# Seventh head pair normalised by GpSimd inside its own unit and turned by DMA, and four blocks of the first product multiplied ahead of their Mish

## The chip, the cores and the metric

The kernel runs on one core of a Trainium2 chip. The metric is the device time of one execution in microseconds, lower is better. A run of this kernel is one program launch on real inputs. The engines are named as the profile names them: PE (TensorE, matrix products and transposes), PEld (its weight loads), DVE (VectorE), ACT (ScalarE), POOL (GpSimd), SP (SyncE, which here only issues DMAs).

## The reference

Attention over 8 batches, 12 heads, 448 positions, head size 64, with a softmax whose denominator has one more term, and then a two-layer network with the Mish function on all 3584 rows:

```python
scale = 1.0 / np.sqrt(q.shape[-1])
scores = scale * np.matmul(q, k.transpose(0, 1, 3, 2))
m = np.max(scores, axis=-1, keepdims=True)
e = np.exp(scores - m)
attn = e / (np.sum(e, axis=-1, keepdims=True) + np.exp(-m) + 1e-09)
attn_out = np.matmul(attn, v)
x = attn_out.transpose(0, 2, 1, 3).reshape(B * S, H * D)     # 3584 x 768
h = x @ w_in                                                 # 768 -> 2048
g = h * np.tanh(np.log1p(np.exp(np.minimum(h, 20.0))))       # Mish
out = g @ w_out                                              # 2048 -> 768
```

Inputs and output are fp32; inside, products take bf16 and sum in fp32.

## The kernel before

**Units.** Heads go in pairs (128 rows of q, k and v transposed together), six pairs to a batch, 48 in all. Pairs 0 to 5 (batch 0) form the head of the program. From then on three pairs make a unit: unit 2 is pairs 6, 7, 8, unit 3 is pairs 9, 10, 11, and so on to unit 15. Each unit has twelve steps (four per pair) and then a Mish part of eight blocks: half of the first product, with Mish, of the batch that is one behind. Unit 2 and unit 3 thus do blocks 0 to 7 and 8 to 15 of batch 0. From unit 4 on, the steps have the second product (`mm2_part`, L443) of earlier batches as filler on PE.

**A step.** `exps` (L298) takes the exponentials of a step's two row tiles on ACT (L306, one tile in a pair's last step), from PSUM into a bf16 buffer `en`, subtracting the row maximum. `scores_ahead` (L239) then lets PE compute scores up to three steps ahead, since there are three PSUM tiles `sc`, each free again after its exponentials. DVE reduces each to the negative maximum (L293). So a step turns around ACT, PE and DVE.

**After a pair.** `denominators` (L319, L323) and `normalise` (L325) divide `en` by the sum: seven row tiles, each one instruction, on DVE (L341) or on POOL (L339). For POOL's part, DVE first copies the reciprocals (L331). Then `en` has to be transposed to `eT`. There are two ways: a DMA transpose issued on SP's queue (L345), or `turn_on_pe` (L350), four turns of seven PE transposes each (L356), with an evacuation by DVE (L360). The list `BY_PE` names the pairs that PE turns: 2, 4, 5, 6, 7. `av_pair` (L368) multiplies `eT` with v (L382), and its result is copied to `xT` (L391), the input of the first product.

**The Mish part.** `mm1_mish` (L399) multiplies one block, six matmuls (L406), into a PSUM bank and takes Mish from it on ACT (L412). Between the blocks stand the denominators and normalisations of the unit's three pairs and the transposes (`transpose_pair`, L193) and evacuations (`evac_qk`; L214, L227, L235) of the next unit's three pairs of q and k. ACT has to load another table for Mish and again for the exponential, once each per unit. Before pairs 13 and 14, DVE clears buffers `qd` (L223, L224).

**Banks and evacuations.** Two PSUM banks `mo` serve the turns, the attention products and the blocks; the second block of each part uses an `sc` tile instead (`spare`). An evacuation is put on a list `late` and issued at the next step (`flush_late`).

**Order.** The schedule is written by hand: each engine runs its instructions in the order in which the code emits them, and so do the DMA queues of SP and POOL. `TURN_AT`, `AV_AT` and `W_AT` give for units 2 and 3 the step at which a turn, an attention product or a weight load is emitted. In unit 2, pair 8 was normalised first (DVE, then DMA), pair 6 after block 3 (DVE, then PE), pair 7 after block 4 (POOL, then PE); the turns of pairs 6 and 7 stood at steps 0 to 6 of unit 3, and their products at steps 5 and 8, that of pair 8 at step 10. The q, k and v loads (`load_pair`, L132) go on SP's queue at steps 0, 3 and 6, their casts to bf16 (L175, L176, L162) on POOL; the weights `w_in` and `w_out` come in pieces issued on POOL (L158).

Of the kernel before, what the change touches and what calls it, by code (L numbers as in the profile page):

```python
# [19 lines left out]
def kernel(  # L20
# [9 lines left out]
    nc = tc.nc  # L30
# [9 lines left out]
    FF_T = d_ff // 128  # L40
    NTILE = 2 * S // 128
    UNITS_PER_B = HP // UNIT_PAIRS
    N_UNITS = B * UNITS_PER_B
    HU = 2 * UNIT_PAIRS
    FF_U = FF_T // UNITS_PER_B
# [155 lines left out]
    def evac_qk(p, act=False):  # L201
        if p >= N_PAIRS:
            return
        (q_ps, k_ps), own = qkT[p]
        mo_free.extend(own)
        qd = q_diag[p % 3]
        kT = qk_pool.tile([128, S], BF16, tag="kT", name="kT")
        if not is_diag(p):
            qT = qd.rearrange("d i h r -> d (i h r)")[:, 0:S]
            qkT[p] = (qT, kT)  # L210
            if act:
                nc.scalar.mul(qT, q_ps[:, 0:S], SCALE)
            else:
                nc.vector.tensor_scalar(  # L214
                    out=qT, in0=q_ps[:, 0:S], scalar1=SCALE, scalar2=None, op0=ALU.mult
                )
            if p >= DIAG_FROM:
                nc.gpsimd.tensor_copy(out=q_rest[0:64, 0, :], in_=qT[0:64, 384:S])
                nc.gpsimd.tensor_copy(out=q_rest[64:128, 1, :], in_=qT[64:128, 0:64])
        else:  # L220
            qkT[p] = (qd, kT)
            if p < DIAG_FROM + 3:
                nc.vector.memset(qd[0:64, :, 1, :], 0.0)  # L223
                nc.vector.memset(qd[64:128, :, 0, :], 0.0)  # L224
# [73 lines left out]
    def exps(idx):  # L298
        p, s = divmod(idx, STEPS)
        if p >= N_PAIRS:  # L300
            return
        st = att[p]
        sc, cols = st.pop(("sc", s))
        rg["used"] -= 1
        for bk, c in enumerate(cols):
            nc.scalar.activation(  # L306
                out=st["en"][:, :, c, 0:SP_],
                in_=sc[:, bk, 0:S].rearrange("q (j c) -> q j c", j=NT),
                func=AF.Exp, bias=st["negm"][:, c : c + 1], scale=1.0,
                accum_out=st["sums"][:, c : c + 1],  # L310
            )
        if s == STEPS - 1 and p < HP:
            nc.scalar.activation(out=st["expm"], in_=st["negm"], func=AF.Exp)
        elif s == STEPS - 1 and p % UNIT_PAIRS == UNIT_PAIRS - 1:
            w = st["whole"]
            nc.scalar.activation(out=w["expm"], in_=w["negm"], func=AF.Exp)
# [8 lines left out]
    def normalise(p, dma=True, on_pool=False, shared=0):  # L325
        st = att[p]
        en = st["en"]
        if on_pool or shared:

            st["rden2"] = st_pool.tile([128, NTILE], FP32, tag="rden2", name="rden2")  # L330
            nc.vector.tensor_copy(out=st["rden2"], in_=st["rden"])  # L331
        for i in range(NTILE):
            pool_does = on_pool or i < shared
            args = dict(
                out=en[:, :, i, 0:SP_], in0=en[:, :, i, 0:SP_],
                scalar1=st["rden2" if pool_does else "rden"][:, i : i + 1],
            )
            if pool_does:
                nc.gpsimd.tensor_scalar(scalar2=1.0, op0=ALU.mult, op1=ALU.mult, **args)  # L339
            else:  # L340
# [55 lines left out]
        del att[p], casted[p], qkT[p]  # L396


    def mm1_mish(b, ff):  # L399
        if ff == 0:  # L400
            gT[b] = gT_pool.tile([128, FF_T, S], BF16, tag="gT", name="gT")
        flush_late()
        spare = ff % FF_U == 1
        h_ps = sc_tiles[0][:, 0, :] if spare else mo_take()
        for dm in range(DM_T):
            nc.tensor.matmul(  # L406
                h_ps[:, 0:S],
                lhsT=w_in_sb[:, dm, ff * 128 : (ff + 1) * 128],
                rhs=xT[b][:, dm, :],
                start=(dm == 0), stop=(dm == DM_T - 1),  # L410
            )
        nc.scalar.activation(out=gT[b][:, ff, :], in_=h_ps[:, 0:S], func=AF.Mish)  # L412
        if not spare:
            mo_free.append(h_ps)
# [78 lines left out]
    for g in range(B // 2):  # L493
# [12 lines left out]
        else:  # L506
# [6 lines left out]
    LEAD = UNIT_PAIRS + 1  # L513
    LOAD_AT = (0, 3, 6)
    LAST_AV_AT = (0, 6, 9)
    HEAD = HP

    BY_PE = (2, 4, HEAD - 1, HEAD, HEAD + 1)
    TURN_AT = (
        {0: [(4, 2)], 1: [(4, 3)], **{3 + j: [(HEAD - 1, j)] for j in range(NT)}},  # L520
        {0: [(HEAD, 0), (HEAD, 1)], 1: [(HEAD, 2)], 2: [(HEAD, 3)],
         3: [(HEAD + 1, 0)], 4: [(HEAD + 1, 1)], 5: [(HEAD + 1, 2)], 6: [(HEAD + 1, 3)]},
    )
    TURN_HEAD = {
        (3, 2): [(2, 0)], (3, 3): [(2, 1)], (4, 0): [(2, 2)], (4, 1): [(2, 3)],
# [1 line left out]
    }  # L527
    AV_HEAD = {(3, 3): 0, (4, 2): 2, (4, 3): 1}
    W_HEAD = {0: 3, 1: 1, 3: 1, 4: 1}
    AV_AT = ({3: 4, 7: 3, 9: 5}, {5: 6, 8: 7, 10: 8})  # L530

    W_AT = ({5: 1, 9: 1}, {1: 1, 4: 1, 5: 1, 7: 1, 9: 1, 11: 1}, {3: 1, 5: 1, 7: 1, 9: 1})
    for which in ("qk", "v"):
        for p in range(UNIT_PAIRS):
            load_pair(p, which)
# [39 lines left out]
    for u in range(UNITS_PER_B, N_UNITS + 2 * UNITS_PER_B):  # L575
# [10 lines left out]
        for n in range(steps):  # L586
# [22 lines left out]
            if u - UNITS_PER_B < len(AV_AT):  # L609
                early = AV_AT[u - UNITS_PER_B]  # L610
                if n in early:
                    av_pair(early[n])
                if u == UNITS_PER_B:
                    for part in TURN_AT[0].get(n, []):
                        turn_on_pe(*part)
            elif u == N_UNITS and n in LAST_AV_AT:
                av_pair(p0 - UNIT_PAIRS + LAST_AV_AT.index(n))
            if u - UNITS_PER_B < len(W_AT):
                load_w(W_AT[u - UNITS_PER_B].get(n, 0))
        assert done == total  # L620
# [63 lines left out]
```

## Time and profile before

| what | us |
|---|---|
| median of 3 runs | 481.12 |
| lowest and highest run | 479.0, 483.71 |
| the profiled execution | 479.95 |
| its span | 478.0 |

The profile is of one execution; its page has the time within the span, and 1.95 us of the execution lie around it. More of the page, the slices of the span (40 of 11.95 us each, a digit is a tenth of busy time) for the engines other than PE, and the costliest groups that the change touches (line, engine, operation, output and input, count, busy us in all and ns of one, and the idle time of the engine before them):

```profile
DVE  4888987968787886878687878788787869420021
ACT  5979678878787888979787878888897978412300
POOL 4877809255514334353535242433535340300000
...
L406 PE MATMUL mo<-xT,w_in_sb 128*128 128x448 bf16 x672 | 137.7, 353 | 0.6 <-DVE xT L391 0.6
L412 ACT ACTIVATE gT<-mo 128x448 bf16<-128x448 f32 x112 | 61.3, 547 | 68.2 <-PE mo L406 68.1
...
L339 POOL TENSOR_SCALAR en<-en,rden 128x448 bf16<-128x448 bf16 x122 | 76.4, 646 | 80.7 <-DVE rden L331 76.9
...
L341 DVE TENSOR_SCALAR en<-en,rden 128x448 bf16<-128x448 bf16 x214 | 58.6, 345 | 0.9
```

The mean of a PE instruction includes the fill of the array; matmuls follow each other closer than their duration. The stages meant below: the head up to 54 us, unit 2's steps to 65.0, its Mish part to 75.3, unit 3's steps to 92.2, its Mish part to 102.9, then unit 4 and on.

### The profile page before, as it was taken

The page shows a single profiled execution, that of the slowest core. Times are in us where ns is not written, and L with a number is a line of the kernel's source. Part 1 is how long each engine was busy: PE and PEld are TensorE (multiplying, and loading weights), DVE is VectorE, ACT ScalarE, POOL GpSimd, SP SyncE. Part 2 cuts the span into 40 slices and gives each one's busy share as a digit, 9 for nine tenths or more (in the row PEclk, how much of TensorE's full clock was granted, in tenths as well). Part 3 has the DMA queues.
Part 4 walks back from the last instruction along what each step waited for, and adds up shares of the span by engine and source line. Part 5 has one row for each costly group of instructions (what it writes and reads, how often), then busy time and mean ns, then how long its engine had stood idle before and what let it go on. Part 6 is the DMA issues. An engine that isn't in the chain of part 4 may idle for free.

```text
span 478.0 us, 8924 instructions
## 1 busy us (share of the span) xinstructions
PE 443.1 (93%) x3064; PEld 248.6 (52%) x3064; DVE 339.1 (71%) x680; ACT 350.0 (73%) x919; POOL 181.1 (38%) x315
## 2 busy tenths in 40 slices
PE   4565888898999999999999999999999999999997
PEld 2233544454655555555555555556555555556565
DVE  4888987968787886878687878788787869420021
ACT  5979678878787888979787878888897978412300
POOL 4877809255514334353535242433535340300000
PEclk9998798899999999999999999999999999999999
DMA  8999969999999989899999999899989595870113
GB/s 228 220 233 220 235 100 234 162 187 238 207 217 276 206 212 219 213 203 246 193 250 182 225 167 228 211 207 234 201 233 212 156 178 127 135 164 24 43 28 105
DMA packets 202381, 90.37 MB, mean 189 GB/s; under 512 B 159072, under 2 KB 198880, under 8 KB 202336
## 3 DMA queue, kind: packets, MB, share of 16 engines
q1 hardware_dynamic: 194848, 83.51, 81.3%
q0 software_dynamic: 7488, 6.29, 8.6%
q8 instruction: 24, 0.39, 0.3%
q14 instruction: 21, 0.17, 0.1%
HBM read 45.61 MB, written 11.01 MB: 118 GB/s over the span
## 4 chain that ended last, share of the span: by engine, by line
PE 76%; ACT 10%; DVE 9%; issue 2%; DMA 1%; POOL 0%; SPq 0%; DVEq 0%; ACTq 0%; POOLq 0%
PE mo L472 26%; PE mo L406 25%; ACT en L306 9%; PE sc L382 6%; DVE negm L293 6%; PE sc L266 5%; PE sc L406 4%; PE sc L193 3%; PE sc L272 2%; PE mo L356 1%; PE mo L382 1%; DVE en L341 1%; PE sc L280 1%; DVE eT L360 1%; DMA k_f<-in_k_dram 1%
## 5 line engine op out<-in xcount | busy, mean ns | idle before, releaser
L306 ACT ACTIVATE en<-sc,negm 128x448 bf16<-128x448 f32 x336 | 209.6, 637 | 26.4 <-DVE xT L391 10.4
L293 DVE TENSOR_REDUCE negm<-sc 128x2 f32<-128x896 f32 x192 | 180.7, 968 | 55.8 <-PE sc L275 26.0
L472 PE MATMUL mo<-w_out_sb,gT 128*128 128x384 bf16 (+1 forms) x912 | 142.3, 301 | 0.0
L406 PE MATMUL mo<-xT,w_in_sb 128*128 128x448 bf16 x672 | 137.7, 353 | 0.6 <-DVE xT L391 0.6
L412 ACT ACTIVATE gT<-mo 128x448 bf16<-128x448 f32 x112 | 61.3, 547 | 68.2 <-PE mo L406 68.1
L472 PEld LDWEIGHTS <-gT 128*128 128x128 bf16 x912 | 84.1, 98 | 48.2 <-issue 5.7
L339 POOL TENSOR_SCALAR en<-en,rden 128x448 bf16<-128x448 bf16 x122 | 76.4, 646 | 80.7 <-DVE rden L331 76.9
L406 PEld LDWEIGHTS <-w_in_sb 128*128 128x128 bf16 x768 | 72.9, 98 | 64.0 <-issue 3.0
L306 ACT ACTIVATION_READ_ACCUMULATOR en<-sc,negm 128x1 f32 x336 | 69.3, 206 | 0.0
L175 POOL CAST q_bf<-q_f 112x512 bf16<-112x512 f32 x47 | 29.0, 617 | 98.4 <-DMA q_f<-in_q_dram 98.0
L341 DVE TENSOR_SCALAR en<-en,rden 128x448 bf16<-128x448 bf16 x214 | 58.6, 345 | 0.9
L459 DVE COPY o_sb<-mo 128x384 f32<-128x384 f32 (+1 forms) x65 | 32.2, 495 | 35.1 <-PE mo L472 34.8
L266 PE MATMUL sc<-kT,qd 128*128 128x448 bf16 x168 | 47.7, 354 | 0.3 <-ACT en L306 0.2
L272 PE MATMUL sc<-kT,qd 64*128 64x448 bf16 x72 | 25.1, 411 | 12.7 <-ACT en L306 11.1
L382 PE MATMUL sc<-eT,v_bf 112*64 112x448 bf16 x288 | 34.1, 357 | 1.9 <-ACT en L306 1.7
L162 POOL CAST v_bf<-v_f 112x512 bf16<-112x512 f32 x48 | 29.5, 616 | 9.7 <-DMA v_f<-in_v_dram 8.8
L382 PEld LDWEIGHTS <-v_bf 112*64 112x64 bf16 x384 | 21.0, 112 | 22.8 <-issue 13.6
L176 POOL CAST k_bf<-k_f 112x512 bf16<-112x512 f32 x47 | 28.9, 616 | 7.5 <-DMA k_f<-in_k_dram 7.0
L227 DVE TENSOR_SCALAR qd<-sc 64x448 bf16<-64x448 bf16 x48 | 18.7, 389 | 11.9 <-PE sc L193 11.2
L266 PEld LDWEIGHTS <-qd 128*128 128x128 bf16 x168 | 16.3, 97 | 18.0 <-issue 9.2
L275 PE MATMUL sc<-kT,qd 64*128 64x448 bf16 x72 | 25.4, 415 | 0.0
L472 PE MATMUL mo<-w_out_sb,mid 128*128 128x384 bf16 x128 | 24.9, 326 | 0.0
(57 smaller groups left out, 340.1 us busy)
## 6 DMA issues: line engine op xcount, KB each, us to landing
q_f<-in_q_dram SPq DMA_DIRECT2D x48, 224.0 KB, 5.1
k_f<-in_k_dram SPq DMA_DIRECT2D x48, 224.0 KB, 5.4
v_f<-in_v_dram SPq DMA_DIRECT2D x48, 224.0 KB, 5.7
w_in_sb<-in_moe_w_in_dram POOLq DMA_DIRECT2D x12, 256.0 KB, 6.1
w_out_sb<-in_moe_w_out_dram POOLq DMA_DIRECT2D x8, 384.0 KB, 7.6
out_dram<-o_sb SPq DMA_DIRECT2D x7, 336.0 KB, 3.3
out_dram<-o_sb SPq DMA_DIRECT2D x8, 288.0 KB, 4.6
out_dram<-o_sb SPq DMA_DIRECT2D x8, 240.0 KB, 2.9
```

Source lines behind the costliest of these rows:

```text
L162: nc.gpsimd.tensor_copy(out=casted[p][2], in_=loaded.pop(p)[2])
L266: nc.tensor.matmul(sc[:, bk, 0:S], lhsT=qT[:, i].rearrange("d h r -> d (h r)"), rhs=kT, start=True, stop=True,)
L272: nc.tensor.matmul(sc[:, 0, 0:S], lhsT=qT[0:64, qa : qa + 128], rhs=kA, start=True, stop=True)
L293: nc.vector.tensor_reduce(out=negm, in_=sc[:, 0 : len(cols), 0:S], axis=AX.X, op=ALU.max, negate=True)
L306: nc.scalar.activation(out=st["en"][:, :, c, 0:SP_], in_=sc[:, bk, 0:S].rearrange("q (j c) -> q j c", j=NT), func=AF.Exp, bias=st["negm"][ ...
L339: nc.gpsimd.tensor_scalar(scalar2=1.0, op0=ALU.mult, op1=ALU.mult, **args)
L341: nc.vector.tensor_scalar(scalar2=None, op0=ALU.mult, **args)
L382: nc.tensor.matmul(av[h * 64 : (h + 1) * 64, 0:S], lhsT=v_bf[:, h, j * D : (j + 1) * D], rhs=e_h, start=(j == 0), stop=(j == NT - 1),)
L406: nc.tensor.matmul(h_ps[:, 0:S], lhsT=w_in_sb[:, dm, ff * 128 : (ff + 1) * 128], rhs=xT[b][:, dm, :], start=(dm == 0), stop=(dm == DM_T - 1),)
L412: nc.scalar.activation(out=gT[b][:, ff, :], in_=h_ps[:, 0:S], func=AF.Mish)
L459: nc.vector.tensor_copy(out=o_sb[:, cols], in_=st["o"][:, 0:n_cols])
L472: nc.tensor.matmul(st["o"][:, 0:n_cols], lhsT=src[:, ff, c0 : c0 + 128], rhs=w_out_sb[:, ff, cols], start=(ff == 0), stop=(ff == FF_T - 1),)
```

## The change

1. Pair 6 (`HEAD`) leaves `BY_PE`. At step 9 of unit 2 its denominators are computed (its own exponential of the negative maximum is added on ACT after its fourth step), POOL normalises it, and a DMA transpose on SP's queue turns it. Pair 8 stays with DVE and DMA; pair 7 is normalised by POOL after block 1 in place of block 4 and is turned by PE, now at steps 1 to 4 of unit 3.
2. The products of pairs 6, 8 and 7 stand at steps 1, 3 and 6 of unit 3, in place of 6, 7, 8 at steps 5, 8, 10.
3. Blocks 8 to 11 of batch 0 are multiplied at steps 5, 7, 8 and 10 of unit 3 (`mm1_ahead`). DVE copies each result to an fp32 tile in SBUF, and in the Mish part ACT takes Mish from there. The Mish part's order becomes 8, 12, 9, 13, 10, 14, 11, 15: one block ready, one multiplied.
4. The clearing of the two `qd` buffers moves from DVE to POOL, at the end of unit 3's steps. One weight load moves from block 2 of unit 2 to its step 9.
5. For pair 0, DVE does its three row tiles before it copies the reciprocals for POOL.

```diff
-            if p < DIAG_FROM + 3:
-                nc.vector.memset(qd[0:64, :, 1, :], 0.0)
-                nc.vector.memset(qd[64:128, :, 0, :], 0.0)
...
-        if s == STEPS - 1 and p < HP:
+        if s == STEPS - 1 and p <= HEAD:
             nc.scalar.activation(out=st["expm"], in_=st["negm"], func=AF.Exp)
...
-        for i in range(NTILE):
+        order = list(range(NTILE))
+        if shared and p == 0:
+            order = order[shared:] + order[:shared]
+        for i in order:
+            if i == 0 and (on_pool or shared):
+                for_pool()
...
+    def mm1_ahead(b, ff):
+        h_ps = mo_take()
+        mm1(b, ff, h_ps)
+        h_sb = o_pool.tile([128, d_model], FP32, tag="o_sb", name="o_sb")
+        h_sbs[b, ff] = h_sb
+        def evac():
+            nc.vector.tensor_copy(out=h_sb[:, 0:S], in_=h_ps[:, 0:S])
+            mo_free.append(h_ps)
+        late.append(evac)
+
+    def mm1_mish(b, ff, spare):
...
+        if (b, ff) in h_sbs:
+            nc.scalar.activation(out=gT[b][:, ff, :], in_=h_sbs.pop((b, ff))[:, 0:S], func=AF.Mish)
+            return
...
-    BY_PE = (2, 4, HEAD - 1, HEAD, HEAD + 1)
+    BY_PE = (2, 4, HEAD - 1, HEAD + 1)
     TURN_AT = (
...
-        {0: [(HEAD, 0), (HEAD, 1)], 1: [(HEAD, 2)], 2: [(HEAD, 3)],
-         3: [(HEAD + 1, 0)], 4: [(HEAD + 1, 1)], 5: [(HEAD + 1, 2)], 6: [(HEAD + 1, 3)]},
+        {1 + j: [(HEAD + 1, j)] for j in range(NT)},
...
-    AV_AT = ({3: 4, 7: 3, 9: 5}, {5: 6, 8: 7, 10: 8})
-    W_AT = ({5: 1, 9: 1}, {1: 1, 4: 1, 5: 1, 7: 1, 9: 1, 11: 1}, {3: 1, 5: 1, 7: 1, 9: 1})
+    AV_AT = ({3: 4, 7: 3, 9: 5}, {1: 6, 3: 8, 6: 7})
+    FIRST_AT = {5: FF_U, 7: FF_U + 1, 8: FF_U + 2, 10: FF_U + 3}
+    SECOND = [ff for i in range(4) for ff in (FF_U + i, FF_U + 4 + i)]
+    W_AT = ({5: 1, 9: 2}, {1: 1, 4: 1, 5: 1, 7: 1, 9: 1, 11: 1}, {3: 1, 5: 1, 7: 1, 9: 1})
...
+                if u == UNITS_PER_B + 1 and n in FIRST_AT:
+                    mm1_ahead(0, FIRST_AT[n])
...
+            if (u, n) == (UNITS_PER_B, 9):
+                denominators(att[HEAD])
+                normalise(HEAD, on_pool=True)
...
+        if u == UNITS_PER_B + 1:
+            for t_ in q_diag[1:]:
+                nc.gpsimd.memset(t_[0:64, :, 1, :], 0.0)
+                nc.gpsimd.memset(t_[64:128, :, 0, :], 0.0)
...
+        if u == UNITS_PER_B:
+            todo = [p0 + 2, None, p0 + 1]
         for f in range(FF_U):
             if moe:
-                mm1_mish(b, w * FF_U + f)
-            if u == UNITS_PER_B and f in (2, 6):
+                mm1_mish(b, SECOND[f] if u == UNITS_PER_B + 1 else w * FF_U + f, spare=f == 1)
+            if u == UNITS_PER_B and f == 6:
                 load_w(1)
...
-            if f == 3:
+            if f == 3 and todo[1]:
                 normalise(todo[1], dma=todo[1] not in BY_PE)
-            if f == 4:
+            if f == (4 if todo[1] else 1):
                 normalise(todo[2], dma=todo[2] not in BY_PE, on_pool=True)
```

More of the change, by code (lines that the diff above doesn't have):

```diff
@@ L42 @@
     UNITS_PER_B = HP // UNIT_PAIRS
+    HEAD = HP
     N_UNITS = B * UNITS_PER_B
@@ L327, in normalise, with for_pool @@
         en = st["en"]
-        if on_pool or shared:
+        def for_pool():
             st["rden2"] = st_pool.tile([128, NTILE], FP32, tag="rden2", name="rden2")
             nc.vector.tensor_copy(out=st["rden2"], in_=st["rden"])
-        for i in range(NTILE):
+        order = list(range(NTILE))
[4 more added lines that the diff above has]
+                for_pool()
             pool_does = on_pool or i < shared
@@ L396, in av_pair, with mm1 @@
         del att[p], casted[p], qkT[p]
[L399 to L404, printed above, removed]
+    def mm1(b, ff, h_ps):
         for dm in range(DM_T):
@@ L411, in mm1_mish @@
             )
+    h_sbs = {}
+    def mm1_ahead(b, ff):
[8 more added lines that the diff above has]
+    def mm1_mish(b, ff, spare):
+        if ff == 0:
+            gT[b] = gT_pool.tile([128, FF_T, S], BF16, tag="gT", name="gT")
+        flush_late()
+        if (b, ff) in h_sbs:
+            nc.scalar.activation(out=gT[b][:, ff, :], in_=h_sbs.pop((b, ff))[:, 0:S], func=AF.Mish)
+            return
+        h_ps = sc_tiles[0][:, 0, :] if spare else mo_take()
+        mm1(b, ff, h_ps)
         nc.scalar.activation(out=gT[b][:, ff, :], in_=h_ps[:, 0:S], func=AF.Mish)
@@ L515 @@
     LAST_AV_AT = (0, 6, 9)
-    HEAD = HP
-    BY_PE = (2, 4, HEAD - 1, HEAD, HEAD + 1)
+    BY_PE = (2, 4, HEAD - 1, HEAD + 1)
     TURN_AT = (
         {0: [(4, 2)], 1: [(4, 3)], **{3 + j: [(HEAD - 1, j)] for j in range(NT)}},
-        {0: [(HEAD, 0), (HEAD, 1)], 1: [(HEAD, 2)], 2: [(HEAD, 3)],
-         3: [(HEAD + 1, 0)], 4: [(HEAD + 1, 1)], 5: [(HEAD + 1, 2)], 6: [(HEAD + 1, 3)]},
+        {1 + j: [(HEAD + 1, j)] for j in range(NT)},
     )
```

## The prediction

> **What bounds the kernel now.** I read the page first (busy shares, then the 40 slices), then a table of busy time by stage, then the chain of waits around 86 to 104 us, then the timeline of single engines there.
>
> ```profile
> PE 443.1 (93%) x3064; PEld 248.6 (52%) x3064; DVE 339.1 (71%) x680; ACT 350.0 (73%) x919; POOL 181.1 (38%) x315
> PE   4565888898999999999999999999999999999997
> PEclk9998798899999999999999999999999999999999
> ```
>
> From the tenth slice on (about 119 us) TensorE has no idle time to speak of; before it, it waits. The change edits only work before 103 us and leaves later work as it is. So the question is when unit 4 begins: what is won or lost there is carried by a full TensorE to the end, nearly one to one. The 28 transposes taken away are worth nothing by themselves if they lay in TensorE's idle time.
>
> The stages (from and to, length, busy time of PE, PEld, DVE, ACT and POOL, granted clock, DMA share, GB/s): unit 2's Mish part, unit 3's steps, unit 3's Mish part, unit 4's steps.
>
> ```profile
> 65.00:75.30 10.30, 10.30 (x77) 5.44 (x76) 7.37 (x23) 6.68 (x12) 3.08 (x5) 1.00 0.67 143
> 75.30:92.20 16.90, 12.59 (x99) 7.41 (x98) 14.69 (x22) 15.14 (x47) 11.39 (x19) 0.80 1.14 214
> 92.20:102.90 10.70, 10.70 (x78) 5.79 (x76) 7.31 (x27) 6.93 (x13) 3.25 (x7) 0.99 0.85 151
> 102.90:119.40 16.50, 14.57 (x98) 8.14 (x97) 14.16 (x19) 15.04 (x45) 9.33 (x16) 1.00 1.09 227
> ```
>
> Both Mish parts are full on PE alone; unit 3's steps are nearly full on DVE and ACT, with PE idle 4.3 of 16.9 us at a mean clock of 0.80. Moving four blocks from a PE-full stage into a stage where PE has room is what the change can win. The chain of waits agrees:
>
> ```profile
> 88.64 2.84 PE mo L382 x16
> 91.48 1.67 PE mo L406 x6
> 93.16 1.13 PE sc L406 x6
> 94.29 0.40 PE sc L193 x8
> 94.68 2.27 PE mo L406 x12
> ```
>
> Every step from 88.64 to 102.3 is PE: two attention products at half clock, then eight blocks at about 1.14 us each (2.27 for two) with three transposed pairs (0.40) between them.
>
> **The change part by part.**
>
> *Unit 3's Mish part.* It ran from the table load at 92.17 to the next at 102.89, 10.7 us. After it, PE has 4 blocks x 1.14 + 3 x 0.40 + 0.66 for three scores = 6.4 us. ACT has the load 1.28, eight Mish at a 0.44 pitch and three copies of kT at 0.42 (starts 120.74, 121.18, 121.60, 122.01) = 6.1. That a Mish reads fp32 from SBUF instead of PSUM is in no row; the rows of 128x448 run 0.53 to 0.65 on ACT from either kind of source, so -0.1 to +0.1 each, and I take 0. DVE has 0.47 for the denominators, two normalisations at 1.81, evacuations 0.39 + 2 x 0.78 and 0.17, 6.2; its four memsets (0.245 each) have gone to GpSimd, idle for 8.29 us before 94.98, where four cost 0.8 (by the 0.20 memset) to 2.6 (by a 0.62 cast): hidden. Three engines near 6.3 do not mesh perfectly: 6.6. Gain 4.1.
>
> *Unit 3's steps.* DVE sets the pace there:
>
> ```profile
> 84.61 0.61 DVE L293 TENSOR_REDUCE negm<-sc 128x1 f32<-128x448 f32 x1
> 85.14 0.61 DVE L360 COPY eT<-mo 112x896 bf16<-112x896 bf16 x1
> 85.68 1.08 DVE L293 TENSOR_REDUCE negm<-sc 128x2 f32<-128x896 f32 x1
> 86.67 0.61 DVE L391 CAST xT<-mo 128x448 bf16<-128x448 f32 x1
> 87.20 0.61 DVE L360 COPY eT<-mo 112x896 bf16<-112x896 bf16 x1
> 87.74 2.61 DVE L293 TENSOR_REDUCE negm<-sc 128x2 f32<-128x896 f32 x3
> ```
>
> Starts follow each other without a gap: 1.0 us per double reduction, 0.53 per copy. Eleven copies stay eleven (four eT of pair 6 out, four h copies in; a 128x448 fp32 copy is between the 0.55 of a 128x384 fp32 copy and the 0.615 of the xT cast: 0.6, pitch 0.53). But their places change. From the reduction at 78.61 to the unit's last reduction (end 90.35) there were seven copies; in the new order there are nine (four eT, three xT, two h): +1.06. Pair 6's product now stands at step 1, when PE has just been idle and runs at half clock (1.71 us for the eight matmuls at 53.13 against 0.95): the evacuation behind it leaves DVE idle some 0.6. Against this, the last exponential began 0.95 after its reduction because ACT had its own queue; that slack goes. Net +0.06 + 1.06 + 0.6 - 0.95, plus some 0.2 of hand-over: +1.0. PE at full clock fits: four blocks at 1.14 come in, four turns of 0.55 to 0.99 go.
>
> *Unit 2.* The new denominators of pair 6 stand on DVE between the last reduction (63.26) and the xT copy of pair 5 (63.79). Their three instructions took 0.51 from first start to the next instruction at 43.07. Behind that copy wait the sixth matmul of the first block (64.46) and all blocks queued behind it, which run without a gap to 74.7: +0.5. The extra exponential of pair 6 (0.23) stands where ACT waits for DVE: 0. GpSimd normalises pair 6 from about 64.9 (seven at 0.62: to 69.2), where it was idle until 72.22.
>
> GpSimd and DVE then normalise side by side. The trace has this in the head, where DVE's third instruction took 0.633 against 0.328 while GpSimd's ran: it waited until GpSimd's ended. So I price pair 8's seven DVE instructions at one per GpSimd instruction, 7 x 0.62 = 4.4 us for 1.81. They end at 70.2, the evacuation behind them at 70.6, and PE's scores that need it were at 70.07, now 70.6: cost 0 by a hair, since the 1.81 us of pair 6 no longer stands on DVE. Pair 7's scalars are copied behind these, so GpSimd starts pair 7 at 70.8 and ends at 75.2 (before: 76.55).
>
> The Trainium skill's page "SBUF — State Buffer", section "Who interferes with whom", says that the two engines share one port pair as an exclusive lock and that the second to issue blocks for the whole instruction; the head's row agrees for DVE, and by the rule GpSimd would block in its turn, which is the third rival below.
>
> *Queues.* SP, in order: pair 6's transpose waits for GpSimd until 69.3, takes 4.2 (as at 67.42), pair 8's follows to 77.7; the loads behind them, at 71.72 before, come 6.0 later. GpSimd waits for them at pair 13's cast, done near 84.3 (3.3 to 4.6 us after issue, as at 108.77; before 81.3); behind it the last w_in piece lands 6.1 to 9.4 later, 90.4 to 93.7, needed by PE near 93.5: 0. Pair 0's reordering starts GpSimd 0.8 later, its transpose 0.8 later, its user stands 6 us after the landing: 0. Pair 6's own transpose lands near 75.8 to 78, its product is at 80.6: 0.
>
> *Unit 4.* The three transposes of unit 3 were issued at 95.03, 99.6 and 104.2 and landed 6.2 later; the products using them ran at 105.67, 111.06 and 115.99: slack 4.4, 5.3, 5.6. Transposes move by +1.5, products by -2.6: slack 0.3, 1.2, 1.5. I take a wait of 0.1.
>
> Sum: +0.5 + 1.0 - 4.1 + 0.1 = -2.5 us. The profiled execution took 479.95 (span 478.0 and 1.95 around it), so 477.5 of its kind; it lay 1.2 under the median of 481.12, against which I state the forecast: 478.6.
>
> **The rivals.**
>
> *No stretch.* DVE's new copies fit into gaps, and unit 2's delay is absorbed in ACT's 1.28 table load: -4.1 to -4.6. For it: ACT idles 2.2 us in unit 3's steps. Against: DVE's gapless starts above. Time 476.7.
>
> *Late transposes in unit 4.* Landing took 9.3 at 121.87 instead of 6.2, with other transfers about; here w_out pieces, issued some 5 us later, would be those. The first product then waits 3.0 beyond its 0.3 slack, the later ones not more: -2.5 + 2.8 = +0.3, 481.4.
>
> *Lock both ways.* GpSimd also waits for DVE (its first instruction beside DVE took 0.725, not 0.639). Seven pairs at 0.62 + 0.25 end at 71.8 and the scores behind run 1.5 late: -1.0, 480.1.
>
> *Half clock through unit 3's steps (slower).* PE now idles from 75.2 to 78.6, longer than the 2.1 us after which the clock showed 0.50 to 0.61 from 78.3 to 81.7; from 46.0 to 54.5 it stayed at 0.50 for 8 us with PE mostly busy. If that holds over the steps, four blocks cost 1.14 more each (4.6), three turns 0.43 (1.3), seven scores 0.2 (1.4), two products 0.54 (1.1): +8.4, nearly all on the path since PE would be full. -2.5 + 8.4 = +5.9, 487. It turns the sign when it holds for over 30% of the stretch, some 3.4 us past 82.4. Against it: PE has no gap over 0.4 us in the new order from 78.6 on.
>
> The Trainium skill's page "TensorE: Matmul & The Clock Gate", section "What's actually happening", says that the clock returns after one busy window of about 3.4 us which runs freely; by that rule, an estimate, the half clock would end between 82 and 85.4 and cost at most 2.5, the whole gain. The chain above has a half-clock stretch end near 92.5 after some 4 us.
>
> **How the numbers follow.** Forecast 0.52, no stretch 0.20, late transposes 0.12, lock 0.07, half clock 0.09. Runs of one kernel spread from 479.0 to 483.71, so 1% (4.8 us) is about what a measurement tells from no change. Faster by over 1% means under 476.3: half of "no stretch" and a sixth of the forecast, 0.19. Slower by over 1% means above 485.9: the half clock and some of the late transposes with the spread, 0.13. Within: 0.68. The range 475.5 to 483.5 takes in all but the half clock and the tails, with the spread of the runs.
>
> **What would show it.** Right: the stretch between the two table loads around unit 3's Mish part falls from 10.7 to about 6.6; the last reduction of unit 3's steps ends near 92.5; the first matmul of the output product at 100.4 instead of 102.89; two transposes on SP's queue back to back from 69.3 and the loads from 77.7. Wrong: a gap before a product in unit 4 that a transpose ends; PEclk at 5 after 85; a gap on PE near 70 to 73; DVE idle in unit 3's steps. The forecast falls if the steps stretch by more than 3 us or not at all.

## The result, and the profile after

| | changed kernel | kernel before, on the same chip |
|---|---|---|
| median of 9 runs each, us | 485.17 | 480.25 |
| lowest and highest, us | 484.28, 487.82 | 479.0, 483.71 |
| ratio, 95% interval | 1.011 (1.0082 to 1.0138) | |
| the profiled execution, its span | 486.29, 484.3 | 479.95, 478.0 |

The change costs 1.1%, about 5 us, where the prediction said 478.6 and gave a range up to 483.5. The page of the changed kernel, its busy shares and the slices for PE and its clock:

```profile
PE 444.0 (92%) x3036; PEld 246.9 (51%) x3036; DVE 341.1 (70%) x672; ACT 350.4 (72%) x920; POOL 186.7 (39%) x326
PE   4565887988879999999999999999999999999996
PEclk9998797999989999999999999999999999999999
```

The sum of PE's work is the same within 1 us, and the clock of unit 3's steps no lower than before. In PE's row the seventh to twelfth slices now read 7, 9, 8, 8, 8, 7 where before they read 8, 8, 9, 8, 9, 9; the twelfth (133 to 145 us) has an 8 in the row of the clock as well, for a 9. The last two of these slices lie in units 4 and 5, which the diff does not touch.

The table by stage of the changed kernel (from and to, length, busy time and instructions of PE, PEld, DVE, ACT and POOL, granted clock, DMA share, GB/s); the lines are unit 2's Mish part, unit 3's steps, its Mish part, unit 4's steps, its Mish part, and unit 5's steps:

```profile
65.30:76.90 11.60, 10.74 (x73) 5.50 (x73) 7.89 (x16) 6.88 (x12) 10.68 (x18) 1.00 0.63 93
76.90:95.20 18.30, 15.47 (x97) 7.45 (x97) 14.36 (x21) 15.30 (x46) 9.24 (x16) 0.81 1.19 227
95.20:102.10 6.90, 6.16 (x51) 3.43 (x50) 6.29 (x23) 6.66 (x14) 1.48 (x5) 1.00 1.35 175
102.10:119.50 17.40, 14.85 (x98) 8.18 (x98) 14.17 (x20) 15.04 (x45) 8.29 (x14) 1.00 1.07 235
119.50:130.30 10.80, 9.56 (x72) 5.13 (x70) 8.24 (x23) 6.89 (x14) 7.20 (x14) 1.00 1.26 207
130.30:151.10 20.80, 18.35 (x114) 9.85 (x113) 14.12 (x19) 15.21 (x45) 5.02 (x9) 0.92 1.10 218
```

The stages begin and end with ACT's table loads. By the exact loads, in us, where M is a Mish part, S a unit's steps and the number the unit:

| | M2 begins | M2 | S3 | M3 | S4 | M4 | S5 | M5 |
|---|---|---|---|---|---|---|---|---|
| before | 64.99 | 10.35 | 16.83 | 10.72 | 16.55 | 9.32 | 16.77 | 9.97 |
| changed | 65.27 | 11.64 | 18.31 | 6.86 | 17.46 | 10.72 | 20.87 | 9.89 |
| difference | +0.28 | +1.29 | +1.48 | -3.86 | +0.91 | +1.40 | +4.10 | -0.08 |

The differences add up to +5.5, and the last table load of the program indeed comes 5.5 us later (412.04 against 406.51). From unit 6 on the stages of the two kernels are alike. The spans of the two profiles differ by some 6.2 us; the other 0.7 lies behind the last matmul (4.0 us to the end for 3.3) and was not followed. So unit 3's Mish part gave what was promised (-3.86 for -4.1), units 2 and 3 gave back 2.8 of it, and units 4 and 5 took 6.4 more. Unit 5 is the largest item. The chain of waits of the changed kernel leads there (start, length, what):

```profile
97.97 7.66 DMA eT<-en
...
120.94 2.88 DVE en L345 x6
123.82 0.07 DVE qd L215
123.89 12.13 DMA eT<-en
...
136.16 0.95 PE sc L386 x8
```

The first DMA transpose of unit 4's pairs is issued at 123.89 and lands 12.1 us later; unit 5's first attention product waits for it. Before, the same transpose was issued at 121.87, took 7.2 us of SP's queue and landed after 9.3, at 131.2, and its product ran at 132.15 without an idle time in front of it:

```profile
132.15 0.95 PE L382 MATMUL sc<-eT,v_bf 112*64 112x448 bf16 x8
```

A stretch of the second product fills PE up to that point. So the first product had a slack of about 1 us, which the prediction does not weigh. The second had none left: its transpose landed at 137.01 and it ran at 137.15. The same stretch of the changed kernel in narrow windows:

```profile
134.00:136.20 2.20, 0.04 (x2) 0.07 (x4) 0.00 (x0) 1.46 (x6) 0.00 (x0) 1.00 1.21 256
136.20:138.00 1.80, 1.80 (x12) 0.90 (x13) 0.48 (x1) 0.00 (x0) 0.00 (x0) 0.80 1.17 218
138.00:140.00 2.00, 2.00 (x8) 0.86 (x6) 1.13 (x3) 0.73 (x2) 0.00 (x0) 0.50 1.08 199
140.00:142.00 2.00, 2.00 (x11) 1.00 (x10) 1.85 (x3) 1.33 (x4) 0.00 (x0) 0.83 1.15 215
```

PE is empty for the 2.45 us of the wait, runs its product at full clock, and then stands at 0.50 from about 137.3 to 140.7: 3.4 us at half clock, which costs 1.7 us of PE's work. 2.45 + 1.7 = 4.15, against 4.10 more in unit 5's steps. The Trainium skill's page "TensorE: Matmul & The Clock Gate", section "What's actually happening", gives a free-running window of about 3.4 us for the clock, and puts the drop after one idle window. The half clock here has that length, but 2.45 us of idle time were enough for it, and the drop came 1.1 us after PE had work again.

Why the transpose takes longer is in SP's queue (start, length, instruction; three transposes each, those of unit 3's pairs and of unit 4's). Before:

```profile
95.03 13.69 SPq L345 DMA_TRANSPOSE eT<-en  x3
...
121.87 16.58 SPq L345 DMA_TRANSPOSE eT<-en  x3
```

Changed:

```profile
97.97 14.35 SPq L349 DMA_TRANSPOSE eT<-en  x3
...
123.89 18.75 SPq L349 DMA_TRANSPOSE eT<-en  x3
```

The second of unit 3's in the kernel before (at 99.91), with no load and no weight piece in flight beside it, takes 4.3 us of the queue and lands after 6.2; three take about 13. Behind unit 3's three stand, in order, nine loads (pairs 16 to 18; from 108.77 before, from 112.36 now), POOL's casts of them, and behind the casts on POOL the last four pieces of `w_out` (issued two at a time, at 115.09 and 118.30 before, at 118.71 and 122.00 now). The last two, before and changed:

```profile
118.30 1.48 POOL L158 DMA_DIRECT2D w_out_sb<-in_moe_w_out_dram  x2
```

```profile
122.00 1.48 POOL L159 DMA_DIRECT2D w_out_sb<-in_moe_w_out_dram  x2
```

When unit 4's first transpose was issued, all nine loads had landed, and of the pieces three were in flight before and four now. Before, the last two were 3.6 us old; now they were 1.9 us old. The last piece landed at 128.2 before and at 133.5 now, and the transpose 3.0 and 2.5 us after it.

### The profile page after: what moved, and what is told of

Same layout as the page of the kernel before. It is cut to its first block, busy times and chain, and to the rows that moved or that the text cites. A ratio compares the mean times of both kernels' runs of the same rounds, so it can differ in the third digit from the quotient of the medians.

```text
span 484.3 us, 8864 instructions
## 1 busy us (share of the span) xinstructions
PE 444.0 (92%) x3036; PEld 246.9 (51%) x3036; DVE 341.1 (70%) x672; ACT 350.4 (72%) x920; POOL 186.7 (39%) x326
## 4 chain that ended last, share of the span: by engine, by line
PE 71%; DVE 12%; ACT 9%; DMA 5%; issue 2%; SPq 0%; DVEq 0%; ACTq 0%
PE mo L496 26%; PE mo L405 22%; ACT en L304 8%; DVE negm L291 6%; PE sc L386 6%; PE sc L264 5%; DMA eT<-en 4%; PE sc L405 3%; DVE en L345 3%; PE sc L194 3%; PE sc L270 2%; PE mo L360 1%; PE mo L386 1%; DVE xT L395 1%; PE sc L278 1%
## 5 line engine op out<-in xcount | busy, mean ns | idle before, releaser
L343 POOL TENSOR_SCALAR en<-en,rden 128x448 bf16<-128x448 bf16 x129 | 80.4, 642 | 70.8 <-DVE rden L328 65.1
L436 ACT ACTIVATE gT<-mo 128x448 bf16<-128x448 f32 x108 | 59.1, 547 | 65.5 <-PE mo L405 65.2
L345 DVE TENSOR_SCALAR en<-en,rden 128x448 bf16<-128x448 bf16 x207 | 60.7, 365 | 0.9
L270 PE MATMUL sc<-kT,qd 64*128 64x448 bf16 x72 | 25.7, 414 | 12.7 <-ACT en L304 10.9
L273 PE MATMUL sc<-kT,qd 64*128 64x448 bf16 x72 | 26.0, 418 | 0.0
L496 PE MATMUL mo<-w_out_sb,mid 128*128 128x384 bf16 x128 | 24.9, 326 | 0.0
```

The costliest lines, as they stand in the source:

```text
L270: nc.tensor.matmul(sc[:, 0, 0:S], lhsT=qT[0:64, qa : qa + 128], rhs=kA, start=True, stop=True)
L496: nc.tensor.matmul(st["o"][:, 0:n_cols], lhsT=src[:, ff, c0 : c0 + 128], rhs=w_out_sb[:, ff, cols], start=(ff == 0), stop=(ff == FF_T - 1),)
```

## The experiments

The first four runs set three theories against each other, named in their expectations: the queue theory (pair 6's new transpose stands ahead of the loads on SP's queue, so they and later transposes come late), the lock theory (GpSimd beside DVE) and the stretch theory (more copies on DVE lengthen unit 3's steps). A fourth possibility is that one half of the change alone carries the loss. After these four came the collision theory: whatever begins later in unit 3 pushes loads and `w_out` pieces into unit 4's first transpose, and unit 5 pays. The runs in the order in which they were made; in each group the kernel before ran on the same chip.

| run | median | before | ratio, 95% interval |
|---|---|---|---|
| e1_ahead_alone | 485.41 | 480.56 | 1.0106 (1.0080 to 1.0133) |
| e2_pair6_alone | 484.34 | 480.56 | 1.0091 (1.0057 to 1.0125) |
| e4_pair6_dve_dma | 483.68 | 480.56 | 1.0058 (1.0038 to 1.0079) |
| e5_loads_first | 504.92 | 480.56 | 1.0495 (1.0464 to 1.0525) |
| e3_no_second_half | 480.79 | 480.25 | 0.9999 (0.9980 to 1.0019) |
| e6_w_early | 482.85 | 480.25 | 1.0052 (1.0025 to 1.0079) |
| e7_before_w_early | 479.12 | 480.25 | 0.9965 (0.9949 to 0.9981) |
| e9_dve_dma_w_early | 480.11 | 480.25 | 0.9997 (0.9975 to 1.0020) |
| e10_before_late_start | 482.20 | 480.02 | 1.0050 (1.0031 to 1.0068) |
| e11_two_ahead_w_early | 479.07 | 480.02 | 0.9985 (0.9973 to 0.9998) |
| e12_three_ahead_w_early | 478.95 | 480.02 | 0.9974 (0.9953 to 0.9994) |
| e13_changed_w_step0 | 492.21 | 480.02 | 1.0253 (1.0222 to 1.0284) |

Their stages, in us, as above:

| | M2 begins | M2 | S3 | M3 | S4 | M4 | S5 | M5 |
|---|---|---|---|---|---|---|---|---|
| e1 | 65.42 | 10.36 | 17.11 | 9.35 | 16.86 | 9.68 | 23.21 | 9.36 |
| e2 | 65.36 | 11.64 | 17.53 | 9.79 | 16.55 | 9.83 | 18.70 | 9.87 |
| e4 | 65.48 | 10.34 | 17.79 | 6.86 | 17.57 | 10.18 | 19.40 | 9.98 |
| e5 | 66.49 | 11.65 | 18.32 | 6.86 | 30.16 | 11.17 | 16.69 | 9.31 |
| e3 | 66.38 | 11.66 | 18.32 | 6.86 | 17.56 | 9.49 | 16.69 | 9.31 |
| e6 | 65.54 | 11.65 | 17.92 | 8.04 | 20.75 | 9.32 | 16.70 | 9.31 |
| e7 | 66.27 | 10.35 | 16.64 | 9.79 | 16.55 | 9.32 | 16.70 | 9.31 |
| e9 | 65.66 | 10.34 | 17.80 | 7.04 | 21.51 | 9.32 | 16.70 | 9.31 |
| e10 | 65.08 | 10.36 | 16.84 | 10.84 | 16.55 | 9.33 | 18.81 | 9.87 |
| e11 | 65.58 | 10.35 | 17.02 | 9.78 | 16.56 | 9.32 | 16.69 | 9.31 |
| e12 | 65.44 | 10.36 | 17.32 | 9.26 | 16.96 | 9.32 | 16.69 | 9.31 |
| e13 | 65.68 | 11.64 | 18.57 | 6.95 | 26.51 | 10.24 | 16.69 | 9.31 |

The moment at which M2 begins scatters by 1.5 us between profiles of programs that are nearly the same up to there; so lengths are compared.

**e1_ahead_alone.** The blocks ahead, without pair 6's new way: pair 6 is back on DVE and PE, all turns and products stand at their old steps, and the blocks at steps 6, 7, 9 and 11. The small moves (the memsets, one weight load, pair 0's order) stay. The two lines that matter:

```diff
-    BY_PE = (2, 4, HEAD - 1, HEAD + 1)
+    BY_PE = (2, 4, HEAD - 1, HEAD, HEAD + 1)
...
-    FIRST_AT = {5: FF_U, 7: FF_U + 1, 8: FF_U + 2, 10: FF_U + 3}
+    FIRST_AT = {6: FF_U, 7: FF_U + 1, 9: FF_U + 2, 11: FF_U + 3}
```

> Pairs 6 and 7 as in the kernel before (DVE and GpSimd in the Mish part, both turned by PE), the four blocks still multiplied ahead, at steps 6, 7, 9 and 11 of unit 3. Queue theory (the extra transpose on SP's queue makes the loads behind it, and through them later transposes, late): nothing on SP's queue moves, so units 4 and 5 keep their 26 us; unit 3's steps grow by 1 to 2 us, its Mish part loses 3.9: 477.5 to 479.5. Lock theory (GpSimd beside DVE): the same. Stretch theory (four more copies on DVE eat the gain): 480.5 to 482. If a shorter Mish part alone makes the transposes late: 482 to 485, with a wait for eT in unit 4 or 5.

It lost as much as the whole change, so the queue theory falls as the one cause: no transpose of pair 6 stands ahead of any load here. Unit 5's steps are the longest of all, 23.21. In its chain the fourth block's evacuation stands on DVE at 95.18, ahead of the denominators, and unit 3's first transpose is issued at 98.56, later than in the changed kernel (97.97). The end of the chain:

```profile
122.41 13.87 DMA eT<-en
...
136.41 1.70 PE sc L386 x8
```

The transpose now lands 13.9 us after its issue, PE waits 4.2, and the product behind it runs at half clock (1.70 in place of 0.95). The last two pieces were issued at 121.92, only 0.5 us ahead of the transpose (122.41).

**e2_pair6_alone.** Pair 6's new way, without blocks ahead.

```diff
-    FIRST_AT = {5: FF_U, 7: FF_U + 1, 8: FF_U + 2, 10: FF_U + 3}
-    SECOND = [ff for i in range(4) for ff in (FF_U + i, FF_U + 4 + i)]
+    FIRST_AT = {}
+    SECOND = list(range(FF_U, 2 * FF_U))
```

> Pair 6 by GpSimd and DMA as in the changed kernel, all eight blocks multiplied in the Mish part. Queue theory: the loads are as late as in the changed kernel but unit 3's Mish part ends some 3 us later, so part of the lateness is hidden: 483 to 487, the wait for eT in unit 5 smaller than 2.5 us. Lock theory: unit 2's Mish part 1.3 longer and nothing else, 481.5 to 482.5. If the blocks ahead are to blame: 479.5 to 481.

Half of the change, and nearly all of the loss again: M2 keeps its +1.29, and unit 5 waits 1.6 us for the first transpose and 0.3 for the third. Both halves fall into the same hole; their losses do not add.

**e4_pair6_dve_dma.** The changed kernel with pair 6 normalised by DVE, as before, and still turned by DMA.

```diff
-            if (u, n) == (UNITS_PER_B, 9):
-                denominators(att[HEAD])
-                normalise(HEAD, on_pool=True)
...
-            todo = [p0 + 2, None, p0 + 1]
+            todo = [p0 + 2, p0, p0 + 1]
...
-    AV_AT = ({3: 4, 7: 3, 9: 5}, {1: 6, 3: 8, 6: 7})
+    AV_AT = ({3: 4, 7: 3, 9: 5}, {1: 8, 3: 6, 6: 7})
```

> Pair 6 normalised by DVE after block 3 as before, but turned by DMA behind pair 8 on SP's queue; blocks ahead as in the changed kernel. Queue theory: still two transposes ahead of the loads, 483 to 486, with a wait for eT in unit 5. Lock theory: unit 2's Mish part is back at 10.4 us and the time is 479 to 481.

This shows what the two engines do to each other in unit 2, though it takes away pair 6's early denominators as well. The timeline of DVE in the changed kernel, pair 8's seven normalisations, and of PE, the transposes of the second pair of q and k (in brackets what it waited for):

```profile
65.94 3.73 DVE L345 TENSOR_SCALAR en<-en,rden 128x448 bf16<-128x448 bf16 x7
```

```profile
70.03 0.36 PE L194 MATMUL sc<-ident,q_bf 112*128 112x112 bf16 x4 [0.56 <-DVE qd L215]
```

In this experiment, with POOL doing none of pair 6:

```profile
66.03 1.81 DVE L345 TENSOR_SCALAR en<-en,rden 128x448 bf16<-128x448 bf16 x7
```

M2 falls from 11.64 back to 10.34. The seven instructions cost 1.9 us more beside POOL's, and the evacuation of the first pair of q and k waits behind them; the second pair's transposes need its tile and ran at 68.45 before. The rows of the two kernels tell the two parts of the 1.29 us apart. The second block of the Mish part began 0.34 us ahead of the table load before (64.65) and 0.23 behind it in the changed kernel (65.50), after the xT copy that the denominators delay: 0.57. The second pair's transposes began 3.46 us after the table load before and 4.76 in the changed kernel, so the remaining 0.7 is the late evacuation. The Trainium skill's page "SBUF — State Buffer", section "Who interferes with whom", lets the later of the two engines block for a whole instruction; DVE's 3.73 for 1.81 agrees, and POOL's own seven (4.38 beside them, 4.33 alone) show next to none of it on its side. The whole kernel still loses 0.6%: unit 3's steps and unit 4 take back 2.8 of M3's 3.86, and unit 5's steps cost 2.6 (19.40), 2.1 for the first transpose and 0.45 for the third.

**e5_loads_first.** The loads of pairs 13 to 15 are issued at step 7 of unit 2, ahead of the two transposes, and every later load one unit earlier.

```diff
+            if u == UNITS_PER_B and n == 7:
+                for p_ in range(3):
+                    load_pair(p0 + LEAD + UNIT_PAIRS + p_)
...
+                if u > UNITS_PER_B:
+                    load_pair(p0 + LOAD_AT.index(n) + LEAD + UNIT_PAIRS)
```

> The changed kernel, with the loads of pairs 13 to 15 put on SP's queue at step 7 of unit 2, ahead of pair 6's transpose, and every later load three pairs ahead (after the cast that frees its buffer). Queue theory: casts no longer wait for loads, the wait for eT in unit 5 goes, 478 to 481. Lock theory: unit 2's 1.3 us remain and the rest too, 484 to 486. Stretch theory: 484 to 486.

The clearest miss. Unit 5 is well (16.69), but unit 3's three transposes took 24.9 us of SP's queue. The first met three loads and two weight pieces in flight (7.4 us, landing after 9.4), and unit 4 waits 2.5 us for it. The third took 13.0 and landed after 17.8, and no load moved beside it until it left the queue: with the loads early, POOL's casts no longer wait, and the four pieces behind them are issued from 110.69 to 114.64, around the third transpose at 111.13. Unit 4 waits 10.5 us for it; unit 6 and every second unit after it take 19.25 us for their steps in place of 16.7, and the time is 24 us worse. That a transpose is delayed by what moves on other queues, not only by what stands ahead of it in its own, is the theory from here on.

**e3_no_second_half.** The changed kernel without the last four pieces of `w_out`. The second product takes the first half of the columns of `w_out` for both halves, so the second half of the weights is never loaded; all else is as in the changed kernel.

```diff
-        for h in range(2):
+        for h in range(1):
...
-                    rhs=w_out_sb[:, ff, cols],
+                    rhs=w_out_sb[:, ff, (q0 % 2) * NQ : (q0 % 2) * NQ + n_cols],
...
-    W_AT = ({5: 1, 9: 2}, {1: 1, 4: 1, 5: 1, 7: 1, 9: 1, 11: 1}, {3: 1, 5: 1, 7: 1, 9: 1})
+    W_AT = ({5: 1, 9: 2}, {1: 1, 4: 1, 5: 1, 7: 1, 9: 1, 11: 1}, {})
```

> The changed kernel without the four loads of the second half of w_out in unit 4; the second product uses the first half of w_out for both halves of the columns, so half of the output columns are others. Collision theory (unit 4's first transpose runs into the late loads of pairs 16 to 18 and these four pieces, 5.6 MB per 13 us): that transpose takes 5 to 7 us of SP's queue in place of 10.0, the wait for eT in unit 5 goes from 2.5 to under 0.5, unit 5's steps from 20.9 to 17 to 18.5: 481 to 482.5. If only the q, k and v loads collide: unit 5 stays over 20, 484.5 to 486.

SP's queue in this kernel, the three transposes of unit 4's pairs:

```profile
123.90 12.99 SPq L349 DMA_TRANSPOSE eT<-en  x3
```

They take 12.99 for 18.75; the first lands after 6.2 for 12.1, and unit 5 falls to 16.69. M4 falls from 10.72 to 9.49 too. The four pieces are thus a necessary part of the loss. What is left of the change is level with the kernel before (0.9999), not faster: M2, S3 and S4 give back 3.8 of M3's 3.86.

**e6_w_early.** All pieces of `w_out` stay. Four more are issued at step 9 of unit 2, so every later piece comes four places earlier and none is left for unit 4.

```diff
-    W_AT = ({5: 1, 9: 2}, {1: 1, 4: 1, 5: 1, 7: 1, 9: 1, 11: 1}, {3: 1, 5: 1, 7: 1, 9: 1})
+    W_AT = ({5: 1, 9: 6}, {1: 1, 4: 1, 5: 1, 7: 1, 9: 1, 11: 1}, {})
```

> The changed kernel with four more weight pieces issued at step 9 of unit 2, when GpSimd and the DMA engines are idle, and none in unit 4. Collision theory: unit 5's steps fall from 20.9 to 17 to 18.5, unit 4's Mish part from 10.7 to about 10: 480 to 482. Otherwise: 484.5 to 486.

Unit 4's Mish part and unit 5 are whole again (9.32, 16.70), but the pieces now meet unit 3's first transpose, with four in flight at its issue for two in the changed kernel: the three transposes took 17.06, and unit 4's steps wait 3.5 us for the first (20.75). The collision was moved, and 0.5% stays, a little above the 480 to 482 that was expected.

**e7_before_w_early.** The same move of pieces in the kernel before.

```diff
-    W_AT = ({5: 1, 9: 1}, {1: 1, 4: 1, 5: 1, 7: 1, 9: 1, 11: 1}, {3: 1, 5: 1, 7: 1, 9: 1})
+    W_AT = ({5: 1, 9: 5}, {1: 1, 4: 1, 5: 1, 7: 1, 9: 1, 11: 1}, {})
```

> The kernel before with the same weight pieces early. Collision theory: its products in unit 5 did not wait, so nothing to win there: 479.5 to 481; the landing of unit 4's first transpose falls from 9.3 to about 7 us. If the pieces in unit 4 cost anything else: below 479.

Faster than both kernels: 0.9965 (0.9949 to 0.9981). Unit 4's three transposes take 13.00 in place of 16.58. The gain lies in M3 (9.79 for 10.72) and M5 (9.31 for 9.97); unit 5's steps change little (16.70 for 16.77), as before had no wait there to lose, only a slack of 1 us.

**e9_dve_dma_w_early.** e4 and e6 together: no interference of DVE and POOL in unit 2, and the pieces early.

> Pair 6 normalised by DVE and turned by DMA, blocks ahead, weight pieces early. Collision theory: unit 2's Mish part 10.3, unit 3's steps 17.8, Mish part 6.9, unit 4 some 1 to 1.5 longer than before, unit 5's steps under 18: 477.5 to 480, below the kernel before. Otherwise as without the early pieces, 483 to 484.

Level with before (0.9997). M3 stays short (7.04) and M2 is that of before, but unit 3's transposes took 16.7 and unit 4 waits 3.1 us (21.51, where 1 to 1.5 more than before was expected): what M3 wins, S4 takes. Against e7, which has the pieces early as well, what is left of the change costs 1 us (480.11 for 479.12).

**e10_before_late_start.** The kernel before, with 16 small memsets on DVE at the start of unit 3's Mish part, so that its normalisations and with them its transposes start later and nothing else changes.

```diff
+                if u == UNITS_PER_B + 1:
+                    for _ in range(16):
+                        nc.vector.memset(spare_sb, 0.0)
```

> The kernel before, with sixteen small memsets on DVE (some 1.8 us) ahead of unit 3's denominators and nothing else. Its Mish part is full on PE and DVE is idle there for over 3 us, so by busy time alone this costs 0 to 0.5 us: 480 to 481. Collision theory: unit 3's three transposes start 1.8 us later, so do the loads of pairs 16 to 18 behind them, and unit 4's first transpose then lands past the 1 us of slack that its product had: unit 5's steps 18 to 20 in place of 16.8, 482 to 484.

The transposes in SP's queue:

```profile
97.18 13.27 SPq L346 DMA_TRANSPOSE eT<-en  x3
...
122.37 18.21 SPq L346 DMA_TRANSPOSE eT<-en  x3
```

Unit 3's first transpose comes 2.15 us later than before, unit 3's Mish part loses 0.12, and unit 5's steps lose 2.04: PE waits 1.0 for the first transpose and 1.0 at the next product (139.43). The view names a reduction on DVE for this second wait, but that reduction ends only after the product has begun; the second transpose landed at 139.30, 0.13 ahead of the product, as the first landed 0.14 ahead of its own. No block ahead and no pair 6 is needed for the loss. With e3 this settles the cause: a later start of unit 3's transposes, together with the pieces behind them. The size here is under half of the changed kernel's, and no half clock follows.

**e11_two_ahead_w_early and e12_three_ahead_w_early.** e1 with the pieces early, and only two or three blocks ahead, none at the last step.

```diff
-    FIRST_AT = {5: FF_U, 7: FF_U + 1, 8: FF_U + 2, 10: FF_U + 3}
+    FIRST_AT = {7: FF_U, 9: FF_U + 1}
...
-    SECOND = [ff for i in range(4) for ff in (FF_U + i, FF_U + 4 + i)]
+    SECOND = [FF_U + i for i in (0, 2, 1, 3, 4, 5, 6, 7)]
```

> The kernel before with the weight pieces early and two blocks (8 and 9) multiplied ahead, at steps 7 and 9 of unit 3. Collision theory: unit 3's transposes start within 1 us of before and unit 4 is free of weight loads, so unit 3's Mish part falls to 7.5 to 8.5 us and what it gains is kept: 477 to 478.5. Stretch theory: unit 3's steps grow by as much: 479 to 480.

> The same with three blocks ahead (8, 9 and 10, at steps 6, 7 and 9). Collision theory: 476.5 to 478.5, if unit 3's transposes still start within 1 us; a wait for eT in unit 4 if they start later: 478.5 to 480.

Both are just under before (0.9985 and 0.9974) and no different from e7, which has no block ahead: two blocks leave M3 where e7 has it (9.78 and 9.79, not the 7.5 to 8.5 that was expected), three bring it to 9.26 and lose that in S3 and S4. The timelines of e7 and e11 show where the two blocks go. In both, PE turns the second pair of q and k 3.69 us after the table load (at 96.95 and 96.64), and four blocks follow. In e7 PE reaches that point without a gap; in e11 it has fewer blocks to do but waits 0.5 us for DVE's evacuation, which stands behind an xT copy at 93.40, the denominators and seven normalisations.

**e13_changed_w_step0.** The changed kernel with its four late pieces at step 0 of unit 4.

```diff
-    W_AT = ({5: 1, 9: 2}, {1: 1, 4: 1, 5: 1, 7: 1, 9: 1, 11: 1}, {3: 1, 5: 1, 7: 1, 9: 1})
+    W_AT = ({5: 1, 9: 2}, {1: 1, 4: 1, 5: 1, 7: 1, 9: 1, 11: 1}, {0: 4})
```

> The changed kernel with the four weight pieces of unit 4 issued at its step 0, behind pair 15's cast and so some 10 us earlier, in place of steps 3, 5, 7 and 9. Collision theory: unit 4's first transpose meets less, its 10.0 us of queue time falls to 5 to 8, unit 5's steps to 17 to 19; the second and third transposes of unit 3 are slowed by some 2 us each and unit 4's steps grow by 0 to 2: 481.5 to 484.

Worse by 2.5%, where 481.5 to 484 was expected. Unit 3's third transpose, with the pieces issued around it (108.5 to 111.6), seen by its source line (time on the queue, issue, then the landing):

```profile
L349 SPq DMA_TRANSPOSE eT<-en x1: 11355/11355/11355, 108.8 to 108.8; - x1
...
DMA to landing us min/median/max: 16.1/16.1/16.1
```

PE waits 8.8 us for it in unit 4 (26.51). Of the places tried for these four pieces in the changed kernel, each meets one of unit 3's or unit 4's transposes: the first of unit 4 (as it is), the first of unit 3 (e6), the third of unit 3 (e13). The stages of the changed kernel have a DMA share of 1.07 to 1.35 from 77 to 130, so a free place is hard to find there.

## Why the prediction was wrong

- *What bounds the kernel.* Read rightly for units 2 and 3. The row of PE is full from the eleventh slice on (119.5 us), not the tenth, which shows an 8; and a 9 leaves up to a tenth of a slice, 1.2 us, unseen. But above all "TensorE has no idle time to speak of" was taken to mean that nothing there could be late. A full row says that no wait shows, not how much room is left until one does; at unit 5's first product that was about 1 us, at its second nothing.
- *Unit 3's Mish part.* Right: 6.86 for a forecast of 6.6, -3.86 for -4.1. The four Mish from SBUF and the memsets on POOL (0.47 to 0.51 each, inside the 0.2 to 0.62 given) cost little: such a Mish took 0.58 to 0.59 us where one from PSUM took 0.53 to 0.55.
- *Unit 3's steps.* The mechanism was right from 86 us on (DVE without gaps, pairs of reductions and copies); from 80 to 86 PE is full at half clock, and DVE idles 1.0 us between its first reduction (80.37) and 86, where 0.6 was given. So the size was a little small: +1.48 for +1.0. The half clock rival came in part. The mean clock was 0.81 for 0.80 before, but the mean hides that PE stood at 0.50 from 79.2 to 86.1 in one piece, where before there were two pieces of 3.4 us (from 78.7 and from 88.9). The sign "PEclk at 5 after 85" was thus met, without the loss that it stood for: the steps grew by 0.5 beyond the forecast, not by the 8.4 of the rival.
- *Unit 2.* The denominators cost what was forecast (0.57 for +0.5). At the normalisation the term was right and the user was wrong. The price of pair 8's normalisation beside POOL was bounded well (4.4 forecast, 3.73 measured; POOL's own seven took 4.38 for 4.33, so the rival "lock both ways" did not come), but it was weighed against the scores that ran at 70.07. Ahead of them on PE stand the transposes of the second pair of q and k, at 68.45 before, which need the tile that the delayed evacuation frees: 70.03 now, which is 0.7 us for the forecast of 0. Together M2 grew by 1.29 for +0.5; in e4, without both, it is back at 10.34.
- *Queues.* "The loads behind them come 6.0 later" held (7.1), and the uses named after it show no wait, as said. The transpose that the same chain of loads, casts and pieces reaches in the next round, unit 4's, was not looked at. M4's +1.40 belongs here: pair 17's late casts on POOL, from 120.25, run beside pair 12's normalisation on DVE (3.71 for 1.81) in the changed kernel, and with the pieces gone or early M4 falls to 9.49 and 9.32.
- *Unit 4.* +0.1 forecast, +0.91 measured: unit 3's first transpose, with two `w_out` pieces in flight, landed after 7.7, not the 6.2 of before, and PE waited 0.77 for it. The rival "late transposes in unit 4" had the mechanism (a landing stretched by `w_out` pieces) in the right words, but mainly at the wrong unit and at too small a price: it put 2.8 us in unit 4, where PE waited 0.77, and the 2.45 of waiting and 1.7 of half clock came in unit 5.
- *The sum.* It ended with unit 4, on the ground that what is won or lost before is carried to the end nearly one to one. That step failed: the sum lacks a term for unit 5, put at 0 on that ground alone, where the runs showed +4.10, from a transpose that lands after 12.1 us in place of 9.3. With M2 and M4 mis-sized by 0.8 and 1.4, S4 by 0.8 and S3 by 0.5 it makes 7.6 of the 8.0 us from -2.5 to +5.5.

The length of unit 5's wait does not follow from the delay of unit 3's first transpose alone (issued at 97.18 for a wait of 1.0 in e10, 97.07 and 1.6 in e2, 96.36 and 2.1 in e4, 98.56 and 4.2 in e1). It follows how recent the last weight pieces are when unit 4's first transpose is issued. The last two (counted from the first of them) were issued 3.6 us earlier in the kernel before, 2.6 in e10, 2.2 in e2, 1.9 in e4 and in the changed kernel, and 0.5 in e1; the transpose took 7.2, 8.9, 9.2, 9.8, 10.0 and 11.8 us of the queue. In all six it landed 2.1 to 3.0 us after the last piece. Loads were in flight at its issue only in e1 (two) and e4 (one). A shorter M3 also moves the transpose towards the pieces, and this gap takes in both.

Two things stay open. The half clock adds 1.7 us in the changed kernel, but waits nearly as long did not bring it elsewhere (2.5 us in e5, 2.1 in e4), and why was not settled. And no version that keeps four blocks ahead and finds the pieces a free place was found, so whether one exists was not shown.

## What to carry to other kernels

A stage that shows no wait can still be microseconds from one: before a stage upstream is sped up or shifted, compare, for each transfer downstream, the landing with the first use, two or three stages on and not only in the next. Where the DMA engines are full, moving a transfer moves a collision; count what else is in flight when a latency-critical transfer is issued. For a value delayed on an engine, look for its first user in the order of the queue, not for the most prominent one.

## What the runs showed of the hardware

- A DMA transpose of one pair took 4.2 us of SP's queue and landed after 6.2 with no load and no weight piece in flight (e3, unit 4's first); beside three or four weight pieces of 384 KB it took 7.2 and 9.3 (before), 10.0 and 12.1 (changed), 11.4 and 16.1 (e13), and 13.0 and 17.8 (e5; in the last two, loads were issued before it landed). The Trainium skill's page "DMA: Bandwidth & Descriptors", section "Queues, rings and completion order", says that each DMA engine takes turns between queues by the packet; the stretch agrees with sharing, but no run here tells it from another cause.
- An idle stretch of 2.45 us on PE was followed, 1.1 us after its end, by 3.4 us at half clock, and one of 3.5 (e6) likewise; after 3.1 (e9) and 4.2 (e1) the half clock began while PE still waited and lasted 6.8. Stretches of 1.0 (e10), 2.1 (e4) and 2.5 us (e5) were not followed by any, their windows showing 1.00 throughout. So the length of the idle stretch alone did not decide it.
- DVE's seven bf16 normalisations took twice their time beside POOL's work (3.73 beside its normalisations, 3.71 beside its casts, 1.81 alone), while POOL's seven took 4.38 for 4.33.
